# Placing two x tiles' transposes around one slot's second products, and bounding VectorE's background ahead of transposes

## The chip, the core and the metric

The kernel runs on one core of one Trainium2 chip. The time is the device time of one launch in microseconds (us), the median of several runs. TensorE multiplies matrices into PSUM, VectorE and ScalarE compute element by element and empty PSUM, GpSimd does small side work, and SyncE issues transfers. Each engine works through its own queue in order and waits on semaphores for the others.

## The reference

`x` is 2048 x 576 in float32. One normalised copy of it feeds an attention with a dilated window and a dense layer with ReLU, and both results are added to `x`.

```python
xn = layernorm(x)                                  # 2048 x 576
q, k, v = split(xn @ wqkv)                         # 32 heads of 18
# a position s sees s, s-2, ..., s-14 (8 keys); positions before 0 are masked
attn = softmax(q . k[s - 2*w] * 18 ** -0.5)
A = (attn . v[s - 2*w]) @ wo                       # 576 x 576
B = relu(xn @ w1) @ w2                             # 576 x 4608, 4608 x 576
out = x + A + B
```

## The kernel before

Each float32 operand of a matmul is split into a high and a low part, and a product takes three terms (high by high, high by low, low by high). `two` (L158, L160, L162) does so for weights: ScalarE copies the high part, VectorE (or, for a few, GpSimd) subtracts it from the source.

The positions are worked in two phases (`ph`) of eight tiles of 128 rows. A phase has 144 slots: 12 chunks of 384 columns of `w1`, and in each chunk 4 pairs of x tiles (`tb`) by 3 blocks of 128 columns (`f`). Slot `n` emits, for all engines, in this order:

- `run_splits`: weights that are due are split.
- `h_two`: TensorE's first products, `x` by `w1`, for the pair of slots two ahead. In an even slot this is the first half (28 matmuls), in an odd one the second (26), and then `h_out` brings the two results out of PSUM: ScalarE writes `hhi` (L559), VectorE writes `hlo` (L562). The results lie in two tiles called `ph` or two called `pm`.
- the work in `todo`, put there by `at`: first products of the attention (`qkv_tile`), loads, statistics, norms, transposes.
- `o_two`: TensorE's second products, `h` by `w2` (24 matmuls, more where `wo` is multiplied in), into four tiles `po`. Every third slot `o_out` adds them to `x` on VectorE (L674).
- the work in `todo_late`, put there by `late`.
- `run_bg`: VectorE's background, which is the attention's element-wise work (`attention` puts it in the queue `bg`: L439 and L442 for the logits, L471 for the products with `v`, L478 for their sums). An operation is taken as long as a running estimate of VectorE's time does not pass TensorE's by more than `margin(n)`.

All matmuls (L125) run as pairs, one on each half of TensorE's rows. PSUM has two tiles `pm`. They serve the pairs of first products, the attention's first products, and all transposes by `turn_rows` (L354), of which one call takes both tiles: 10 small matmuls.

Transposes come from two places. `make_xt_rows` turns a normalised tile of the next phase's `x`; ScalarE (L340, L341) and VectorE (L342, L343) then empty the two tiles `pm` into `xT`, one half each. `wo_parts` turns a finished tile of the attention's result; ScalarE (L520) and VectorE (L521, L522) empty it into a tile `k` and a tile `xn`, and slots 266, 269, 272 and 275 multiply them by `wo`.

The steps of the next phase's tiles stand in `XT_STEPS`, one row for each tile: the slots of its load, its statistics (`stats`), its norm (`norm`, three ScalarE instructions, L283, L284, L289) and its transposes, counted from slot 132. So tile 0 is transposed in slot 135, tiles 1 and 2 both in slot 136, tile 3 in slot 142, tiles 4 and 5 in slots 144 and 145, tiles 6 and 7 in 147 and 148. `wo_parts` of the second phase stand in slots 264, 265, 267, 268, 270, 271, 273 and 274.

`busy_m` is the set of all slots that use `pm` for transposes or for the attention's first products. `margin` reads it, and so does `h_two`, which then doesn't take `pm`. In each phase the attention's last unit leaves its background to the slots just before and among the `wo_parts`.

Of the kernel before, what the change touches and what calls it, by code (L numbers as in the profile page):

```python
# [33 lines left out]

XT_STEPS = (
    (-6, 0, 1, 3), (-5, 0, 2, 4), (-3, 1, 3, 4), (4, 6, 7, 10),
    (4, 6, 8, 12), (7, 9, 10, 13), (8, 12, 13, 15), (10, 13, 14, 16),
)
WO_STEPS = (-2, -1)
HEADW = (-9, -8, -7, -6, -5, -4)  # L40
# [16 lines left out]
def tile_body(ctx: ExitStack, tc: tile.TileContext, x, wqkv, wo, w1, w2, out):  # L57
# [440 lines left out]
    def run_bg(margin):  # L498

        ran = False  # L500
        while bg and t["dve"] + bg[0][0] / 960.0 <= t["pe"] + margin and not (ran and bg[0][0] == 0):
            n, f, a = bg.popleft()
            f(*a)
            if n:
                ran = True
                dve(n)
# [179 lines left out]
    def at(n, f, *a):  # L686
        todo.setdefault(n, []).append((f, a))
# [3 lines left out]
    def late(n, f, *a):  # L691
        todo_late.setdefault(n, []).append((f, a))

    plan = []
    busy_m = set()
    for ph in range(NPH):
        b = ph * SPP
        for c in range(NCH):
            for f in range(C):
                s = b + c * SPC + f  # L700
                first = ph == c == 0
                plan.append((HEADW[f] if first else s + (-5, -5, -4)[f], w1_task, ((ph, c, f), c * C + f)))
                plan.append((HEADW[3 + f] if first else s + (-3, -2, -2)[f], w2_task, ((ph, c, f), c * C + f)))
        for u in range(NU):
            s = b + UNIT0[ph] + u * UNIT_STEP
            plan.append((s - 5, wq_tasks, ((ph, u), u)))
            for i in range(NI):
                at(s + i, qkv_tile, ph, u, i)
                busy_m.add(s + i)
            at(s + NI, halos, ph, u)  # L710
            late(s + NI + 1, attention, ph, u)
        plan.append((b + WO_CHUNK * SPC - 6, wo_tasks, (ph,)))
        for i in range(NI):
            z = b + WO_CHUNK * SPC + C * (i // 2) + C - 1
            at(z + WO_STEPS[i % 2], wo_parts, ph, i)
            busy_m.add(z + WO_STEPS[i % 2])
        if ph + 1 < NPH:
            e = b + SPP - SPC
            for i in range(NI):
                load, sums, normed, parts = (e + k for k in XT_STEPS[i])  # L720
                at(load, load_x, ph + 1, i)
                at(sums, stats, ph + 1, i, False, True)
                at(normed, norm, ph + 1, i, True)
                at(parts, make_xt_rows, ph + 1, i)
                busy_m.add(e + XT_STEPS[i][-1])
    for step, f, a in sorted(plan, key=lambda z: z[0]):
        if f in (wq_tasks, wo_tasks):
# [85 lines left out]
        late((4, 4, 6, 7)[tb], twin, tb)  # L813
    def margin(n):

        odd, qkv = n % 2 == 0, n + 1 in busy_m
        due = sum(z[0] <= n + 1 for z in (*staged, *tasks))
        if slots[n][3] == 1:
            return (1.8 if odd else 2.7 + 2.4 * qkv) - 0.8 * due + 1.6 * (odd and qkv)
        return (2.5 if odd else 3.5 + 2.4 * qkv) - 0.8 * due + 1.6 * (odd and qkv)  # L820

    for n in range(FIRST, len(slots)):
        if n == ROW0:
            AHEAD["n"] = 4
        run_splits(n)
        g = n - n % 2 + LAG
        if n < ROW0:
            h_mm(n + LAG)
        elif g < len(slots):
            h_two(g, n % 2 == 1)  # L830
        for f, a in todo.pop(n, []):
            f(*a)
        if ROW0 - 1 <= n < len(slots) - C:
            o_two(n)
        else:
            o_mm(n, n != HALVED)
        if n == HALVED:
            o_out(n, (0,))
        for f, a in todo_late.pop(n, []):
            f(*a)  # L840
        if n == HALVED:
            o_out(n, (1,))
        run_bg(margin(n))
# [27 lines left out]
```

## Time and profile before

| what | value |
|---|---|
| median of 3 runs | 1162.11 us (1159.17 to 1163.46) |
| the profiled execution | 1162.3 us, span 1160.5 us |
| TensorE busy | 1150.2 us, 99% of the span |
| VectorE busy | 795.4 us, 69% |
| ScalarE busy | 295.4 us, 25% |
| granted TensorE clock, mean | 0.997 of full speed |

The profile comes from one execution. PE is TensorE, PEld its loading of weights, DVE is VectorE, ACT is ScalarE, POOL is GpSimd, SP is SyncE. "L354" is line 354 of the kernel. The ends of matmuls are modelled, so short waits between them can hide in what counts as busy, and the time from one start to another is the better measure. The granted clock is the share of full speed that the hardware gave TensorE.

### The profile page before, as it was taken

Reading aid. Unit: us, or ns where it says so; the run is one execution under the profiler, and the core shown is the slowest. Engines: PE = TensorE matmul, PEld = TensorE weight load, DVE = VectorE, ACT = ScalarE, POOL = GpSimd, SP = SyncE. Lnnn points to the kernel's source line nnn. Section 1 sums busy time; section 2 is a strip of 40 time slices with the busy share of each in tenths; the row PEclk is TensorE's granted clock in tenths of the full one; section 3 lists DMA queues with packets and bytes.
Section 4 is the critical chain, followed back from the end, with each engine's and each line's share of the span. In section 5 each row is a group of like instructions: output and inputs, shape, how many; then the busy total and the mean of one; then the engine's idle time right before and its main releaser. Section 6 shows DMA issues by size and latency. Waiting matters only on the chain.

```text
span 1160.5 us, 38715 instructions
## 1 busy us (share of the span) xinstructions
PE 1150.2 (99%) x17334; PEld 1143.6 (99%) x17334; DVE 795.4 (69%) x1465; ACT 295.4 (25%) x796; POOL 55.7 (5%) x80
## 2 busy tenths in 40 slices
PE   9999999999999999999999999999999999999998
PEld 8999999999999999999999999999999999999998
DVE  7427787877787789534564178868868877896333
ACT  5322222221222222222552122222222222231110
POOL 3200000000000000000010000000000000011000
PEclk9999999999999999999999999999999999999999
DMA  6302312221221212301333033032121303221002
GB/s 185 99 21 80 85 35 66 77 66 47 72 68 52 77 39 59 116 25 44 113 96 97 2 100 93 16 92 70 47 65 48 96 14 100 56 80 51 12 2 84
DMA packets 85238, 76.75 MB, mean 66 GB/s; under 512 B 6624, under 2 KB 68832, under 8 KB 85072
## 3 DMA queue, kind: packets, MB, share of 16 engines
q1 hardware_dynamic: 84640, 73.82, 22.3%
q8 instruction: 136, 2.23, 0.8%
q10 hardware_dynamic: 432, 0.46, 0.1%
q14 instruction: 30, 0.25, 0.1%
HBM read 61.34 MB, written 4.72 MB: 57 GB/s over the span
## 4 chain that ended last, share of the span: by engine, by line
PE 97%; DVE 1%; ACT 1%; issue 0%; DMA 0%; POOL 0%; DVEq 0%; ACTq 0%
PE po L125 43%; PE pm L125 26%; PE ph L125 25%; PE ph L115 1%; PE po L115 1%; PE pm L354 1%; DVE x L674 0%; PE pm L302 0%; DMA x<-in_x 0%; PE pm L115 0%; ACT xn L283 0%; DVE bst L263 0%; DVE pr L471 0%; DVE hlo L562 0%; ACT xT L307 0%
## 5 line engine op out<-in xcount | busy, mean ns | idle before, releaser
L125 PE MATMUL po<-w2t,hhi 64*128 64x256 f32 (+1 forms) x4448 | 449.4, 293 | 0.0
L125 PEld LDWEIGHTS po<-w2t,hhi 64*128 64x128 f32 x4448 | 359.0, 185 | 0.6
L125 PE MATMUL po<-w2t,hlo 64*128 64x256 f32 (+1 forms) x2224 | 334.8, 291 | 0.0
L125 PE MATMUL ph<-xT,w1t 64*128 64x256 f32 x5076 | 324.8, 275 | 0.0
L125 PEld LDWEIGHTS ph<-xT,w1t 64*128 64x128 f32 x5076 | 313.5, 185 | 0.7 <-DVE hlo L562 0.2
L674 DVE TENSOR_TENSOR x<-po,x 128x320 f32<-128x320 f32 (+1 forms) x384 | 149.7, 449 | 174.3 <-PE po L125 171.6
L125 PEld LDWEIGHTS po<-w2t,hlo 64*128 64x128 f32 x2224 | 217.7, 186 | 0.0
L125 PE MATMUL pm<-wq,xT 64*128 64x432 f32 x1728 | 179.3, 354 | 0.0
L559 ACT ACTIVATE hhi<-ph 128x256 fp32r<-128x256 f32 x197 | 65.4, 381 | 421.4 <-PE ph L125 409.2
L125 PEld LDWEIGHTS pm<-wq,xT 64*128 64x128 f32 x1728 | 159.9, 184 | 3.3
L125 PE MATMUL pm<-xT,w1t 64*128 64x256 f32 x2430 | 153.4, 273 | 0.0
L125 PEld LDWEIGHTS pm<-xT,w1t 64*128 64x128 f32 x2430 | 148.3, 184 | 0.0
L562 DVE SCALAR_TENSOR_TENSOR hlo<-ph,hhi 128x256 fp32r<-128x256 f32 x197 | 74.5, 417 | 105.7 <-ACT hhi L559 105.6
L439 DVE TENSOR_TENSOR pr<-qo,k 128x1152 f32<-128x1152 f32 x64 | 85.6, 1349 | 4.1 <-DMA k<-k 4.1
L559 ACT ACTIVATE hhi<-pm 128x256 fp32r<-128x256 f32 x91 | 30.0, 382 | 222.1 <-PE pm L125 222.1
L471 DVE TENSOR_TENSOR pr<-lg,v 128x1152 f32<-128x1152 f32 x64 | 84.7, 1349 | 0.2
L442 DVE TENSOR_REDUCE lg<-pr 128x64 f32<-128x1152 f32 x64 | 84.8, 1342 | 0.0
L478 DVE TENSOR_TENSOR pr<-pr 128x288 f32<-128x288 f32 (+1 forms) x128 | 69.9, 597 | 0.0
L162 DVE TENSOR_TENSOR w2t<-st,w2t 128x576 fp32r<-128x576 f32 x72 | 53.8, 747 | 9.8 <-ACT w2t L158 9.6
L562 DVE SCALAR_TENSOR_TENSOR hlo<-pm,hhi 128x256 fp32r<-128x256 f32 x91 | 34.3, 418 | 37.2 <-ACT hhi L559 36.2
L162 DVE TENSOR_TENSOR w1t<-st,w1t 128x640 fp32r<-128x640 f32 x70 | 57.2, 817 | 3.5 <-ACT w1t L158 3.1
L406 ACT ACTIVATE k<-pm 128x144 f32<-128x144 f32 x64 | 19.3, 302 | 146.8 <-PE pm L125 119.5
(86 smaller groups left out, 716.1 us busy)
## 6 DMA issues: line engine op xcount, KB each, us to landing
st<-in_w SPq DMA_DIRECT2D x72, 288.0 KB, 3.0
st<-in_w SPq DMA_DIRECT2D x72, 256.0 KB, 3.0
st<-in_wqkv SPq DMA_DIRECT2D x32, 216.0 KB, 3.0
st<-in_w SPq DMA_DIRECT2D x144, 32.0 KB, 2.7
out<-x SPq DMA_DIRECT2D x15, 288.0 KB, 2.4
x<-in_x SPq DMA_DIRECT2D x14, 288.0 KB, 4.2
k<-k SPq DMA_DIRECT2D x8, 441.0 KB, 3.9
v<-v SPq DMA_DIRECT2D x8, 441.0 KB, 4.5
```

The source lines that it names most:

```text
L115: nc.tensor.matmul(o, l, r, start=start, stop=stop)
L125: ins = nc.tensor.matmul(o, l[z], r[z], start=start, stop=stop)
L162: nc.vector.tensor_tensor(lo, src, f32(hi), op=ALU.subtract)
L354: nc.tensor.transpose(pt[:, k], src[rows, k * P : (k + 1) * P], ident[rows, rows])
L406: nc.scalar.activation(k[:, W - 1 + j, :], pq[:, 1, :], AF.Copy)
L439: nc.vector.tensor_tensor(pr[i], q, window(k, i), op=ALU.mult)
L442: nc.vector.tensor_reduce(lg[:, i], pr.pop(i).rearrange(heads, d=Dh), axis=AX.X, op=ALU.add)
L471: nc.vector.tensor_tensor(pr[i].rearrange(heads, d=Dh), e, window(v, i).rearrange(heads, d=Dh), op=ALU.mult)
L478: nc.vector.tensor_tensor(o, z[:, 0:n], z[:, n : 2 * n], op=ALU.add)
L559: nc.scalar.activation(hi, pt, AF.Relu)
L562: nc.vector.scalar_tensor_tensor(lo, pt, 0.0, f32(hi), op0=ALU.max, op1=ALU.subtract)
L674: nc.vector.tensor_tensor(acc[:, cols], PO[k, h], acc[:, cols], op=ALU.add)
```

## The change

Three edits, each a line or two.

- Where two tiles have their transposes in the same slot, the second one's go to `todo_late`, behind that slot's second products. This holds for tile 2 in slot 136 alone.
- The norm of tile 5 moves from slot 142 to slot 143.
- `margin(n)` treats only slots with the attention's first products as before. Ahead of any other slot in `busy_m` (those with transposes) it is 1.4.

```diff
-    (4, 6, 8, 12), (7, 9, 10, 13), (8, 12, 13, 15), (10, 13, 14, 16),
+    (4, 6, 8, 12), (7, 9, 11, 13), (8, 12, 13, 15), (10, 13, 14, 16),
 ...
+    qkv_slots = set()
 ...
                 at(s + i, qkv_tile, ph, u, i)
                 busy_m.add(s + i)
+                qkv_slots.add(s + i)
 ...
                 at(normed, norm, ph + 1, i, True)
-                at(parts, make_xt_rows, ph + 1, i)
+                (late if i and XT_STEPS[i - 1][-1] == XT_STEPS[i][-1] else at)(parts, make_xt_rows, ph + 1, i)
                 busy_m.add(e + XT_STEPS[i][-1])
 ...
     def margin(n):
-        odd, qkv = n % 2 == 0, n + 1 in busy_m
+        odd, qkv = n % 2 == 0, n + 1 in qkv_slots
+        if n + 1 in busy_m and not qkv:
+            return 1.4
         due = sum(z[0] <= n + 1 for z in (*staged, *tasks))
         if slots[n][3] == 1:
             return (1.8 if odd else 2.7 + 2.4 * qkv) - 0.8 * due + 1.6 * (odd and qkv)
         return (2.5 if odd else 3.5 + 2.4 * qkv) - 0.8 * due + 1.6 * (odd and qkv)
```

In the order in which the engines' queues are then written, no instruction is added or removed. TensorE's differs in slot 136 alone. ScalarE's differs by the one norm. VectorE's differs in slots 264 to 268 alone (elsewhere no background is left where the new `margin` holds, or none comes out otherwise):

```
before                                     after
L478 x2, L478 x2 (sums of tiles 4, 5)      w2t split
L471 x2 (products of tiles 6, 7)           tile 0 of wo_parts: L521, L522 x2
w2t split                                  L478 x2, L478 x2 (sums of tiles 4, 5)
tile 0 of wo_parts: L521, L522 x2          hlo x2
L478 (sum)                                 tile 1 of wo_parts
hlo x2                                     L471 (product of tile 6)
tile 1 of wo_parts                         L674 x4
L674 x4                                    hlo x2
L478 x5 (sums of tiles 6, 7)               tile 2, tile 3 of wo_parts
hlo x2                                     L471 (product of tile 7)
tile 2, tile 3 of wo_parts                 L478 x6 (sums of tiles 6, 7)
```

## The prediction

> **What bounds the kernel now.** I read the page's shares first, then the chain of waits that ended last, then TensorE's own waits, and then the order of time around those waits on four engines.
>
> ```profile
> PE 1150.2 (99%) x17334; PEld 1143.6 (99%) x17334; DVE 795.4 (69%) x1465; ACT 295.4 (25%) x796; POOL 55.7 (5%) x80
> PE 97%; DVE 1%; ACT 1%; issue 0%; DMA 0%; POOL 0%; DVEq 0%; ACTq 0%
> PE pm L354 <- DVE xT L343: 1.9, 2, 1.4
> PE pm L354 <- DVE xn L522: 1.7, 2, 1.3
> ```
>
> TensorE is busy for 1150.2 of 1160.5 us, and the chain is 97% TensorE. The change adds and removes no matmul, so only the time in which TensorE stands, or runs slowly, can come back. The last two rows (total us, times, longest us) say where it stands in mid-kernel: twice ahead of transposes at L354, each time because VectorE has not yet emptied the PSUM tile `pm` that the transposes write. That is 3.6 us, and by itself only 0.3%. The order of time shows more. Columns are start, duration, engine, line, tiles, count; a duration includes a modelled tail, so I measure from start to start.
>
> ```profile
> 556.24 0.48 PE L125 MATMUL po<-w2t,hhi 64*128 64x256 f32 x4
> ...
> 557.91 1.76 PE L125 MATMUL ph<-xT,w1t 64*128 64x256 f32 x28
> 559.50 0.47 PE L354 MATMUL pm<-ident,xn 64*128 64x64 f32 x10
> 561.39 0.24 PE L354 MATMUL pm<-ident,xn 64*128 64x64 f32 x1 [1.42 <-DVE xT L343]
> 562.08 0.74 PE L354 MATMUL pm<-ident,xn 64*128 64x64 f32 x9 [0.45 <-DVE xT L343]
> 562.53 0.82 PE L125 MATMUL po<-w2t,hhi 64*128 64x256 f32 x4
> ...
> 565.55 1.68 PE L125 MATMUL ph<-xT,w1t 64*128 64x256 f32 x26
> ```
>
> This is slot 136. Its first products of `h` (28 matmuls) take 559.50 - 557.91 = 1.59 us, then both x tiles 1 and 2 are transposed back to back, then come its second products (24 matmuls on `po`). In the slot before, those 24 took 557.91 - 556.24 = 1.67 us; behind the wait they take 565.55 - 562.53 = 3.02. The other wait looks alike, at slot 265 (transposes of attention tile 1):
>
> ```profile
> 1052.34 1.67 PE L125 MATMUL ph<-xT,w1t 64*128 64x256 f32 x26
> 1055.30 0.24 PE L354 MATMUL pm<-ident,qo 64*128 64x64 f32 x1 [1.29 <-DVE xn L522]
> 1055.99 0.50 PE L354 MATMUL pm<-ident,qo 64*128 64x64 f32 x9 [0.45 <-DVE xn L522]
> 1056.27 0.51 PE L125 MATMUL po<-w2t,hhi 64*128 64x256 f32 x4
> ...
> 1058.65 2.67 PE L125 MATMUL ph<-xT,w1t 64*128 64x256 f32 x28
> 1061.11 0.44 PE L125 MATMUL po<-w2t,hhi 64*128 64x256 f32 x4
> ```
>
> Behind it, second products take 2.38 us and the next first products 2.46 instead of 1.59. The windows view gives the reason. The last three columns are granted clock, DMA share, GB/s:
>
> ```profile
> 562.10:562.20 0.10, 0.10 (x3) 0.10 (x5) 0.00 (x0) 0.00 (x0) 0.00 (x0) 0.65 0.70 276
> 565.50:565.60 0.10, 0.10 (x5) 0.10 (x4) 0.00 (x0) 0.00 (x0) 0.00 (x0) 0.79 0.00 0
> 1057.00:1057.10 0.10, 0.10 (x6) 0.10 (x4) 0.10 (x2) 0.10 (x1) 0.00 (x0) 0.80 0.00 0
> 1060.40:1060.50 0.10, 0.10 (x5) 0.10 (x4) 0.00 (x0) 0.00 (x0) 0.00 (x0) 0.63 0.00 0
> 5.00:10.00 5.00, 3.86 (x26) 3.05 (x25) 3.49 (x10) 4.32 (x8) 3.34 (x5) 1.00 0.86 244
> ```
>
> The clock falls at about 562.1 and returns at about 565.5; it falls at 1057.1 and returns at 1060.4: 3.4 us both times, and 495 us apart, 145 times 3.41. So it looks as if the clock is decided on a fixed grid of 3.41 us by what TensorE did in one such window, and costs half the window when it falls. Each gap thus costs twice: the standing, then the slow matmuls. The last row is for later: 1.14 us idle in 5 us at the kernel's head, clock 1.00.
>
> **Slot 136: the transposes of tile 2 move behind the second products.** In the changed order TensorE goes on at 559.50 + 0.28 (ten transposes, from 1055.99 to 1056.27) = 559.78 with the 24 second products, until 561.45. What then lets the transposes of tile 2 start is VectorE's emptying of tile 1, two halves:
>
> ```profile
> 561.01 0.23 DVE L343 TENSOR_TENSOR xT<-pm,xT 64x64 fp32r<-64x64 f32 x1
> ...
> 561.71 0.23 DVE L343 TENSOR_TENSOR xT<-pm,xT 64x64 fp32r<-64x64 f32 x1
> ```
>
> The halves end at 561.24 and 561.94, and TensorE went on 0.15 us behind each (561.39, 562.08). The change does not speed these up: they hang on ScalarE's copies of tile 1, which keep their place. So the first transpose goes at 561.45 at once and the second still waits until 562.08. A rest of 562.08 - 561.45 = 0.63 us stays. The standing falls from 562.08 - 559.78 = 2.30 to 0.63: **1.67 us back**. The next products of `h` then start at 562.08 + 0.28 = 562.36 if the clock holds, against 565.55, so together 3.19 come back and **the clock's part is 1.52**. Cover: tile 2's own copies now end later relative to TensorE. Tile 1's ended 561.94 - 559.78 = 2.2 us behind its transposes; so counted, tile 2's end at 562.36 + 2.2 = 564.5, and their `pm` is next written by slot 138's first products, at 562.36 + 1.49 + 1.67 = 565.5 (1.49 for 26 matmuls, of the 1.59 for 28). That leaves 1.0 us; if it were gone, `pm` would be waited for there. VectorE and ScalarE keep their queue order here, and no DMA moves.
>
> **Slot 265: VectorE's background.** What VectorE did while TensorE waited:
>
> ```profile
> 1051.21 2.66 DVE L471 TENSOR_TENSOR pr<-lg,v 128x1152 f32<-128x1152 f32 x2
> ...
> 1055.62 0.23 DVE L522 TENSOR_TENSOR xn<-pm,k 64x64 fp32r<-64x64 f32 x1
> ```
>
> Two background products of 1.33 us stood ahead of the emptying (L521, L522) of attention tile 0, with a weight split between. `margin` gave 5.9 and 4.1 at the ends of slots 263 and 264, less 0.8 for each weight due; it is now 1.4, and the planned order puts that tile's four instructions straight behind the weight split, ahead of all of this background. The emptying ended at 1055.85; without the 2.66 us alone it ends by 1053.2. TensorE is ready for the transposes at 1052.34 + 1.49 = 1053.83, so it waits for nothing. Standing removed: 1055.99 - 1053.83 = **2.16 us**. Slow matmuls: (2.38 - 1.67) + (2.46 - 1.59) = **1.58 us**. The background does not vanish: one L471 now runs in slot 265, another with six sums (L478) behind the emptying of tile 3 in slot 268. What is late next there is the pair `hlo` behind that block:
>
> ```profile
> L471 DVE TENSOR_TENSOR pr<-lg,v 128x1152 f32<-128x1152 f32 x64 | 84.7, 1349 | 0.2
> L478 DVE TENSOR_TENSOR pr<-pr 128x288 f32<-128x288 f32 (+1 forms) x128 | 69.9, 597 | 0.0
> 1077.34 0.23 DVE L522 TENSOR_TENSOR xn<-pm,k 64x64 fp32r<-64x64 f32 x1
> 1085.18 0.76 DVE L674 TENSOR_TENSOR x<-po,x 128x256 f32<-128x256 f32 x2 [5.17 <-PE po L125]
> ```
>
> The block is at most 1.35 + 6 x 0.60 = 4.9 us. From 1077.57 to VectorE's next bound work at 1085.18 are 7.6 us, so it fits with 2.7 to spare, and `hlo` (0.76) too. Cost nothing; without that cover, up to 4.9.
>
> **Norm of tile 5 one slot later.** ScalarE's three instructions of this norm move from ahead of slot 143's `hhi` to behind it.
>
> ```profile
> 586.26 0.42 PE L125 MATMUL po<-w2t,hhi 64*128 64x256 f32 x4
> 588.01 2.20 PE L125 MATMUL ph<-xT,w1t 64*128 64x256 f32 x28
> 589.96 0.46 PE L354 MATMUL pm<-ident,xn 64*128 64x64 f32 x8
> 586.04 0.67 ACT L158 ACTIVATE w2t<-st 128x576 fp32r<-128x576 f32 x1
> 587.53 0.76 DVE L562 SCALAR_TENSOR_TENSOR hlo<-ph,hhi 128x256 fp32r<-128x256 f32 x2
> ```
>
> Second and first products took 589.96 - 586.26 = 3.70, against 1.67 + 1.59 = 3.26: a hidden loss of 0.44 us, as `ph` was freed by `hlo` only at 588.29. `hlo` was late because ScalarE's norm delayed the weight split (586.04), and VectorE's half of that split stood ahead of `hlo`. With the norm away the split is done early and `hlo` ends about 0.6 earlier. **I take 0.4 back**, bounds 0 and 0.44. The norm's transposes stand two slots on, some 6.5 us by these rows, and nothing else reads it: it would have to end later than that to be felt.
>
> **Sum.** 3.19 + 3.74 + 0.4 = 7.3 us. Against the profiled execution's 1162.3 (span 1160.5 and 1.8 around it) that gives **1155.0**. The median of the runs shown, 1162.11, is 0.2 below that execution, so I keep 1155.0. The lowest run, 1159.17, is 3.1 below the profiled one, which is just the clock's part (1.52 + 1.58): it may be an execution in which the grid cut both gaps and the clock held. There only 4.2 come back, which again ends at 1155.0. This supports the forecast, but is an inference.
>
> **The rivals.** (a) The 0.63 us left in slot 136 still lowers the clock. Against it: the 1.14 us idle at the head left it at 1.00; for it: nobody has shown the limit between 1.14 and the 2.16 that did lower it. Price 1.5: 1156.5. (b) The slow spells are not caused by these gaps and come anyway: then only 1.67 + 2.16 + 0.4 = 4.2 come back, 1158.1. The Trainium skill speaks for it: "TensorE: Matmul & The Clock Gate", section "What's actually happening", has the half clock come after at least one idle window of about 3.4 us, and by that rule gaps of some 2.2 us would not lower it. The trace agrees with the page's half rate and with its free-running window of 3413 ns, but here the clock fell right behind the only two gaps of this kind, which speaks against the rule's limit. (c) The change does not reach the waits: a transposed tile still meets a VectorE that is late, and everything stays: 1162. Against it stands the planned order, which moves exactly the named instructions. (d) Slower: the background, held back in slots 263 to 267, is paid out ahead of later evictions, and transposes of slots 270 to 274 wait in its place. It decides once the block exceeds the 7.6 us found above; each such wait costs what slot 265's did, 3.74, and four of them give 1155.0 + 15.0 = 1170.0. At 4.9 us the block is far from it.
>
> **How the numbers follow.** A measurement of this kernel tells about 0.5% (5.8 us) from no change, so "faster" means below 1156.3. Forecast 0.74, its own range 1153.0 to 1157.0 (the runs shown spread by 4.3, half of it either side); (a) 0.10; (b) 0.08; (c) 0.04; (d) 0.04. The range from 1153.0 to 1158.3 takes in the forecast, (a) and (b) and leaves out about 0.15. Faster: four fifths of the forecast and half of (a), 0.65; slower 0.03, the rest 0.32.
>
> **What would show it.** Right: no TensorE wait at L354 for L522, one of about 0.45 us for L343; granted clock 1.00 from 40 us on; the 24 second products behind slot 265's transposes at 1.67 us; slot 143's `hlo` ahead of TensorE. Wrong: a spell of clock 0.50 behind slot 136, a wait of TensorE for `hlo` or `xT` in slots 137 to 139 or 268 to 271, or a time above 1158.3.

## The result and the profile after

The changed kernel takes **1157.73 us** (median of 6, 1154.82 to 1158.04) against 1162.11 for the kernel before (median of 6 as well, 1159.17 to 1163.46): ratio 0.9962, 95% interval 0.9947 to 0.9978. It is faster by 0.4%, and less than the 0.5% set as the bound for "faster". The forecast was 1155.0 with a range of 1153.0 to 1158.3.

The profiled execution took 1154.82 us (span 1153.0), 7.5 less than the profiled one before, where the sum had said 7.3. The median fell by 4.4 only. Executions of both kernels fall into two groups some 3 us apart, and the two medians are not made up of the same ones: of the changed kernel the profiled execution is in the lower group and the five others, at 1157.54 to 1158.04, are in the upper one.

The page's first lines, and TensorE's waits (engine, line, waited for: us in total, times, longest us):

```profile
span 1153.0 us, 38714 instructions
PE 1145.1 (99%) x17334; PEld 1139.6 (99%) x17334; DVE 795.9 (69%) x1465; ACT 295.6 (26%) x796; POOL 53.4 (5%) x80
...
PE pm L354 <- DVE xT L343: 0.4, 1, 0.4
```

The two waits of 1.9 and 1.7 us have become one of 0.4. No wait for L522 is left. TensorE's order of time at slot 136 (start, duration, engine, line, tiles, count):

```profile
557.82 1.76 PE L125 MATMUL ph<-xT,w1t 64*128 64x256 f32 x28
559.41 0.47 PE L354 MATMUL pm<-ident,xn 64*128 64x64 f32 x10
559.69 0.47 PE L125 MATMUL po<-w2t,hhi 64*128 64x256 f32 x4
...
561.33 0.22 PE L354 MATMUL pm<-ident,xn 64*128 64x64 f32 x1
561.99 0.49 PE L354 MATMUL pm<-ident,xn 64*128 64x64 f32 x9 [0.44 <-DVE xT L343]
562.27 1.81 PE L125 MATMUL ph<-xT,w1t 64*128 64x256 f32 x26
```

Tile 1's transposes are followed at once by the second products. Tile 2's first transpose goes at 561.33 and the second waits until 561.99. The next products start at 562.27; this execution was 0.09 us ahead of the other already, so the forecast of 562.36 is met exactly. Slot 265 and slots 143 and 144:

```profile
1048.65 1.68 PE L125 MATMUL ph<-xT,w1t 64*128 64x256 f32 x26
1050.14 0.50 PE L354 MATMUL pm<-ident,qo 64*128 64x64 f32 x10
1050.42 0.51 PE L125 MATMUL po<-w2t,hhi 64*128 64x256 f32 x4
...
1052.10 1.79 PE L125 MATMUL ph<-xT,w1t 64*128 64x256 f32 x28
```

```profile
583.05 0.41 PE L125 MATMUL po<-w2t,hhi 64*128 64x256 f32 x4
...
584.63 1.81 PE L125 MATMUL ph<-xT,w1t 64*128 64x256 f32 x28
586.25 0.49 PE L354 MATMUL pm<-ident,xn 64*128 64x64 f32 x10
```

The transposes of slot 265 wait for nothing, and the second products behind them take 1052.10 - 1050.42 = 1.68 us, where they took 2.38. Slot 143's second and slot 144's first products take 586.25 - 583.05 = 3.20 us, where they took 3.70. The windows view around both old gaps shows the clock (third column from the right) at 1.00:

```profile
558.00:564.00 6.00, 5.56 (x100) 5.41 (x100) 2.73 (x9) 3.22 (x11) 0.00 (x0) 1.00 0.38 101
1046.00:1052.00 6.00, 6.00 (x110) 6.00 (x108) 4.86 (x15) 2.08 (x6) 0.45 (x2) 1.00 0.27 79
```

### The profile page after: what moved, and what is told of

Same layout as the page of the kernel before. It is cut to its first block, busy times and chain, and to the rows that moved or that the text cites. A ratio compares the mean times of both kernels' runs of the same rounds, so it can differ in the third digit from the quotient of the medians.

```text
span 1153.0 us, 38714 instructions
## 1 busy us (share of the span) xinstructions
PE 1145.1 (99%) x17334; PEld 1139.6 (99%) x17334; DVE 795.9 (69%) x1465; ACT 295.6 (26%) x796; POOL 53.4 (5%) x80
## 4 chain that ended last, share of the span: by engine, by line
PE 97%; DVE 1%; issue 1%; DMA 1%; ACT 1%; POOL 0%; DVEq 0%; POOLq 0%; ACTq 0%
PE po L125 43%; PE pm L125 27%; PE ph L125 25%; PE pm L354 1%; PE po L115 0%; PE ph L115 0%; DMA x<-in_x 0%; DMA st<-in_w 0%; DMA st<-in_wqkv 0%; DVE bst L263 0%; POOL rstd L270 0%; DVE x L674 0%; ACT xn L283 0%; DVE w2t L162 0%; PE pm L302 0%
## 5 line engine op out<-in xcount | busy, mean ns | idle before, releaser
L674 DVE TENSOR_TENSOR x<-po,x 128x320 f32<-128x320 f32 (+1 forms) x384 | 149.7, 449 | 169.1 <-PE po L125 166.4
```

Source lines behind the costliest of these rows:

```text
L674: nc.vector.tensor_tensor(acc[:, cols], PO[k, h], acc[:, cols], op=ALU.add)
```

## The experiments

Two things had to be settled: whether each part of the sum belongs to its edit, and where the other 3 us of the median come from. "The lower group" and "the upper group" are the two groups of times. Each run gives the mean granted clock of each execution; one half-clock spell of 3.41 us in mid-kernel brings it to 0.998, sometimes 0.999, two to 0.997 or 0.996; the group and the spells together give the time.

### The changed kernel again

No edit.

> The changed kernel itself, unchanged, to see where its executions differ: its profiled execution took 1154.82 us, its other five 1157.5 to 1158.0. My theory: the 3 us lie in the kernel's head (the first 45 us), where the clock starts at half rate and turns full at some point of a fixed grid; from 45 us on every execution runs alike. Then the times again fall into 1154 to 1158, and a profiled execution above 1156 shows its extra time ahead of 45 us and a granted clock of 1.00 from there to the last matmul. Rival: a half-clock spell behind the 0.63 us that is left in slot 136 comes in most executions; then a profiled execution above 1156 shows a clock of 0.50 near 562 us.

Median 1157.93 us against 1163.62 of the kernel before (23 executions on the same chip), ratio 0.9949 (0.9937 to 0.9962). The profiled execution took 1155.21, the four others 1157.80 to 1158.14, all with clock 1.000: the rival of a spell behind slot 136 falls. But the profiled execution was again of the lower group, so it did not show where the 3 us lie; the theory that they lie in the kernel's head is tested by a trace of the upper group further down.

The kernel before shows the same groups, and the clock sorts its executions. On this chip and the next: at 1.000, about 1159.2 or 1162.2; at 0.998, about 1160.8 or 1163.9; at 0.997, about 1162.3 or 1165.3. So a spell costs 1.6 to 1.7 us, and both groups exist without the change. The profiled execution of before, with its two spells, is of the lower group (1159.2 and two spells of 1.6): 1162.3 there and a median of 1162.11 agree by accident.

### The late transposes alone

```diff
-                at(parts, make_xt_rows, ph + 1, i)
+                (late if i and XT_STEPS[i - 1][-1] == XT_STEPS[i][-1] else at)(parts, make_xt_rows, ph + 1, i)
```

> The kernel before with one edit of the change: tile 2's transposes behind slot 136's second products. My theory: TensorE's time up to slot 138 is 1.67 us shorter where the clock did not fall there before, 3.2 us where it did; slot 265 keeps its wait of 1.7 us and, in an execution whose grid does not cut that gap, its half-clock spell of 3.4 us. Profiled execution 1159.1 against 1162.3, or 1157.5 if the clock holds at slot 265 too. Rival (the half-clock spells come whatever TensorE waits for): a spell of 0.50 still stands near 562 us and only 1.7 us come back.

Median 1158.11 us, ratio 0.9956 (0.9945 to 0.9968); profiled 1157.82, near the 1157.5 expected where the clock holds at both places. TensorE reaches slot 138 3.1 us earlier than in the profiled execution of before, whose clock had fallen there. Slot 265 keeps its wait, and the clock holds there. The windows are those of the clock's grid; the first number behind the length is TensorE's busy time:

```profile
1052.30 0.24 PE L354 MATMUL pm<-ident,qo 64*128 64x64 f32 x1 [1.32 <-DVE xn L522]
1053.00 0.49 PE L354 MATMUL pm<-ident,qo 64*128 64x64 f32 x9 [0.46 <-DVE xn L522]
...
1048.44:1051.85 3.41, 2.54 (x42) 2.34 (x39) 3.41 (x4) 0.89 (x3) 2.52 (x2) 1.00 0.01 1
1051.85:1055.26 3.41, 2.50 (x40) 2.43 (x42) 3.24 (x10) 0.77 (x2) 0.00 (x0) 1.00 0.32 87
```

The grid cut this gap into two halves, and neither window lost enough. All five executions but one (1159.34, clock 0.998) are within 0.3 us; had one of them been of the upper group, it would have stood near 1161.

### The bound on the background alone

```diff
+        if n + 1 in busy_m and not qkv:
+            return 1.4
```

(with `qkv` read from the attention's slots, as in the change)

> The kernel before with one edit of the change: the bound of 1.4 on VectorE's background. My theory: slot 265's wait goes (2.16 us) and with it any half-clock spell there (1.6 us); slot 136 keeps its waits of 1.4 and 0.45 us. Profiled execution 1158.6, with a spell of 0.50 near 562 us if the grid does not cut that gap. Rival (spells come anyhow): a spell of 0.50 stands near 1054 us without a wait ahead of it.

Median 1159.76 us, ratio 0.9970 (0.9960 to 0.9981); 12 executions spread over four places: three at 1156.9 to 1157.2, two near 1158.5, three near 1159.9, four near 1161.6, as two groups with and without one spell must. The profiled one took 1157.17, not the 1158.6 expected with a spell near 562 us: no wait in slot 265, both waits in slot 136, and the clock held there because the grid cut that gap too:

```profile
558.29:561.70 3.41, 1.99 (x39) 1.88 (x36) 1.38 (x5) 2.25 (x7) 0.00 (x0) 1.00 0.34 92
561.70:565.11 3.41, 2.96 (x50) 2.85 (x52) 1.76 (x6) 0.97 (x4) 0.00 (x0) 1.00 0.31 87
```

So the standing time comes back where its edit is, each time, and the clock's part only where the clock had fallen. In neither trace is there a spell where the gap is gone, so the rivals of both runs fall.

### The later norm alone

```diff
-    (4, 6, 8, 12), (7, 9, 10, 13), (8, 12, 13, 15), (10, 13, 14, 16),
+    (4, 6, 8, 12), (7, 9, 11, 13), (8, 12, 13, 15), (10, 13, 14, 16),
```

> The kernel before with one edit of the change: the norm of tile 5 one slot later. My theory: the first products of slot 144 start 0.4 us earlier relative to slot 142, nothing else moves, and the time does not tell it from the kernel before (ratio 0.998 to 1.002). Rival: the norm's delay costs its transposes in slot 145 a wait, and the slot is no earlier.

Median 1161.52 us, ratio 0.9982 (0.9974 to 0.9991). Slot 143's second and slot 144's first products:

```profile
584.81 0.41 PE L125 MATMUL po<-w2t,hhi 64*128 64x256 f32 x4
...
586.39 1.77 PE L125 MATMUL ph<-xT,w1t 64*128 64x256 f32 x28
587.98 0.48 PE L354 MATMUL pm<-ident,xn 64*128 64x64 f32 x10
```

587.98 - 584.81 = 3.17 us instead of 3.70: the norm's edit brings 0.5, and no wait shows at slot 145's transposes. The medians differ by more (2.1 us), but they mix groups and spells. This trace is also the only one of an execution that its time puts into the upper group (1161.52). Its clock is 1.00 up to 1158 us and it has no wait that the others lack. It loses 2.9 us between 608 and 1043 us, spread over that whole time, so not in the kernel's head as I had supposed. The windows view, this kernel first, then the kernel before:

```profile
700.00:800.00 100.00, 100.00 (x1500) 100.00 (x1498) 79.18 (x132) 24.58 (x71) 2.75 (x3) 1.00 0.22 62
800.00:900.00 100.00, 100.00 (x1502) 100.00 (x1500) 80.07 (x134) 23.73 (x68) 2.74 (x3) 1.00 0.23 63
```

```profile
700.00:800.00 100.00, 100.00 (x1511) 99.84 (x1510) 79.89 (x131) 23.54 (x68) 2.75 (x3) 1.00 0.22 61
800.00:900.00 100.00, 100.00 (x1510) 99.84 (x1508) 80.67 (x135) 24.70 (x70) 2.74 (x3) 1.00 0.23 64
```

1500 matmuls in 100 us instead of 1511: some 0.7% less. Read start by start, the two matmuls of a pair (one on each row half) start mostly 5 to 50 ns apart there, and the distance changes from pair to pair; the other traces so far keep a steady 3 or 10 ns. The next theory takes it for a larger distance that lasts.

### A fresh start of both row halves

```diff
+    def drain():
+        tc.add_manual_dep(nc.tensor.nop().ins, LAST[0].ins.name, SYNC, reason="both row halves start anew")
...
+    for n in (150, 152):
+        at(n, drain)
```

(`LAST[0]` is the last matmul issued)

> The changed kernel, with a wait in slots 150 and 152: TensorE's second products there start only when its first products are done, so both row halves start anew. Theory S (skew): most executions of the changed kernel take 3 us more than its profiled one because TensorE's two row halves run the second phase 13 to 49 ns apart instead of 3 to 9, as the norm-only kernel's trace shows (it loses 2.9 us between 608 and 1043 us, evenly, at full clock), and a fresh start near 620 us puts them right: every execution at 1155.0 to 1156.0 (two waits cost 0.2 to 0.5 us). Rival D: the 3 us come from something that the start of both halves does not touch (transfers, the taking of the profile): executions stay at 1157.5 to 1158.5. Rival R: the skew is drawn anew at each start: executions fall into both groups.

Median 1156.35 us of 9, ratio 0.9957 (0.9941 to 0.9973): five at 1155.5 to 1156.4, four at 1158.4 to 1158.8. That is as rival R has it. Five of nine in the lower group, against two of seven in the next run on the same chip, which has no such wait, is too few to say that the wait helps. The two waits themselves cost 0.8 us by this trace (more than the 0.2 to 0.5 expected): from slot 146 to slot 160 it takes 61.36 us, and the changed kernel's second trace 60.60.

### Tile 2's transposes one slot later still

```diff
-    (-6, 0, 1, 3), (-5, 0, 2, 4), (-3, 1, 3, 4), (4, 6, 7, 10),
+    (-6, 0, 1, 3), (-5, 0, 2, 4), (-3, 1, 3, 5), (4, 6, 7, 10),
```

> The changed kernel with tile 2's transposes one slot later still, in slot 137 behind its first products. My theory of the 0.63 us that is left in slot 136: tile 1's copies end 2.2 us behind its transposes, and first products (1.49 us) more lie between now, so no wait is left at L343 and TensorE is 0.6 us earlier at slot 138. Rival: tile 2's copies now stand ahead of the sums of slot 137 on VectorE, and the second products of slot 138 wait for these: the 0.6 us are lost again. Either way the time stays within 0.1% of the changed kernel.

Median 1157.55 us, ratio 0.9956 (0.9939 to 0.9973); lower group 1154.5, upper 1157.5 to 1157.8. The wait for L343 is gone, and the rival came with it. TensorE and VectorE in slot 138:

```profile
566.55 0.45 PE L125 MATMUL po<-w2t,hhi 64*128 64x256 f32 x4
566.78 0.33 PE L125 MATMUL po<-w2t,hlo 64*128 64x256 f32 x2
566.90 0.96 PE L125 MATMUL po<-w2t,hhi 64*128 64x320 f32 x4
...
568.61 1.67 PE L125 MATMUL ph<-xT,w1t 64*128 64x256 f32 x26
565.69 1.55 DVE L674 TENSOR_TENSOR x<-po,x 128x256 f32<-128x256 f32 x4
```

Second products of 568.61 - 566.55 = 2.06 us instead of 1.6: VectorE's copies of tile 2 now stand ahead of its sums (L674, ending at 567.2), and TensorE's matmuls on the two `po` that are summed last (the `64x320` rows) wait for these, hidden in a duration of 0.96 instead of 0.47. Of the 0.63 us, 0.2 are still there at slot 140.

### Pauses of known length

The pauses stand in 19 slots; each adds GpSimd instructions that TensorE waits for, so the time as such says nothing.

```diff
+    def pause(k):
+        for j in range(k):
+            z = nc.gpsimd.memset(pause_tile, 0.0)
+            if j == 0:
+                tc.add_manual_dep(z.ins, LAST[0].ins.name, SYNC, reason="pause starts behind the matmuls")
+        tc.add_manual_dep(nc.tensor.nop().ins, z.ins.name, SYNC, reason="pause ends")
...
+        at(n, pause, 3 + j)
```

> The changed kernel with 19 pauses of TensorE in the first phase, in every fourth slot outside the attention's first products, each as long as a chain of 3 to 21 small GpSimd instructions (about 0.7 to 3.5 us). It measures the clock by itself. My theory: the clock is decided on a fixed grid of 3.41 us, and falls to half for one window where a window had more idle time than some limit between 1.1 and 1.7 us; so pauses under 1.1 us never lower it, long ones do for 3.41 us, and between 1.2 and 2.2 us it hangs on how the grid cuts the pause. Rival (a rule of one whole idle window): only pauses of 3.4 us and more lower it.

The pauses came out at 1.0 to 4.6 us, measured from the last start ahead of a pause to the first behind it. Each window is one of the clock's grid, and the row behind it, where there is one, the next:

```profile
192.06:195.47 3.41, 2.10 (x32) 2.13 (x34) 1.26 (x1) 0.00 (x0) 0.86 (x7) 1.00 0.25 76
205.71:209.12 3.41, 1.67 (x28) 1.49 (x26) 0.52 (x1) 0.00 (x0) 1.10 (x8) 1.00 0.24 65
209.12:212.53 3.41, 3.41 (x59) 3.41 (x58) 2.93 (x8) 1.14 (x3) 0.00 (x0) 1.00 0.02 5
...
219.37:222.78 3.41, 1.47 (x28) 1.30 (x24) 3.41 (x6) 0.00 (x0) 1.24 (x9) 1.00 0.02 6
222.78:226.19 3.41, 3.41 (x29) 3.41 (x31) 0.76 (x1) 0.00 (x0) 0.00 (x0) 0.50 0.30 65
...
297.87:301.28 3.41, 2.28 (x38) 2.07 (x35) 1.61 (x3) 0.00 (x0) 0.71 (x6) 1.00 0.85 241
301.28:304.69 3.41, 2.21 (x34) 2.24 (x36) 1.29 (x2) 0.00 (x0) 0.81 (x6) 1.00 0.02 7
304.69:308.10 3.41, 3.41 (x60) 3.41 (x59) 1.80 (x5) 1.29 (x3) 0.00 (x0) 1.00 0.03 7
```

In this trace a window with 1.47 us busy lowers the clock for the whole next one, and a window with 1.67 does not. A pause of 2.2 us that lies in one window (219.37) costs a spell, one of 2.6 us that is cut in two (297.87, 301.28) costs none. All ten pauses from 2.8 us on lowered it; each left a window with at most 1.18 us busy. The limit that I expected, 1.1 to 1.7 us idle, was somewhat low; the rule of a whole idle window falls.

The two gaps of the kernel before bound the limit from the other side. Each of their windows is followed by the half-clock one:

```profile
558.72:562.13 3.41, 1.54 (x31) 1.32 (x28) 1.30 (x4) 1.72 (x6) 0.00 (x0) 1.00 0.42 100
562.13:565.54 3.41, 3.41 (x33) 3.41 (x35) 1.30 (x4) 0.97 (x4) 0.00 (x0) 0.50 0.16 64
1053.65:1057.06 3.41, 1.67 (x30) 1.39 (x28) 3.29 (x9) 1.22 (x4) 0.32 (x1) 1.00 0.31 87
1057.06:1060.47 3.41, 3.41 (x34) 3.41 (x33) 1.57 (x6) 0.21 (x1) 0.00 (x0) 0.50 0.02 5
```

Here a window with 1.67 us lowered the clock; in the pauses' trace one with the same 1.67 did not. As the ends of matmuls are modelled, the busy time of a window is not good to the last digit; the traces place the limit near 1.67 us of work and no closer.

### One more small matmul on one row half

```diff
+            if g == 154:
+                o, l, r, start, stop, n = runs[0][0]
+                nc.tensor.matmul(o[:, 0:64], l[0:64], r[0:64, 0:64], start=True, stop=True)
```

> The changed kernel with one more small matmul (64 columns, about 27 ns, its result written over by the next) on the first row half alone, ahead of slot 152's first products. Theory S (TensorE's two row halves keep the distance at which they last were set, and 13 to 49 ns cost about 3 us over the second phase): the trace shows another distance than 3 or 9 ns from about 625 us on, and its phase runs slower by up to 3 us, without a wait and at full clock; the shares of the two groups of times (about 1155 and 1158) change. Rival D (the 3 us have nothing to do with the distance): distance changed, second phase as long as before; two groups as in the changed kernel.

The same on the second half (`runs[1][0]`, rows 64 to 127):

> The same with the small matmul on the second row half. Theory S: the distance changes the other way, so that one of the two kernels has more slow executions than the changed kernel and the other fewer, or both more; a profiled execution near 1158 shows a distance over 13 ns through the second phase, one near 1155 a distance of 3 or 9. Rival D: no such link between distance and time in these traces.

And the changed kernel beside them:

> The changed kernel once more as the control for the two. Either theory: times in two groups near 1155 and 1158, three quarters of them in the upper; half of the lower group's distance to the kernel before (4.2 us, group by group) from the waits that went, none from the clock in executions of either that held it.

Medians 1154.97, 1154.91 and 1154.94 us against 1160.71, ratios 0.9952, 0.9951 and 0.9951 (0.9938 to 0.9963 for the control). On this chip no execution of any kernel is of the upper group, which no expectation had foreseen: all 15 of these three lie within 1154.7 and 1155.2, so the shares of the groups could not be compared. In the first trace the pairs start 3 ns apart, a distance that other runs have too. In the second trace the pairs start 23 ns apart through the whole second phase, and it runs as fast as ever, 1510 matmuls in 100 us:

```profile
800.00:900.00 100.00, 100.00 (x1510) 100.00 (x1509) 79.73 (x132) 24.77 (x70) 2.74 (x3) 1.00 0.24 66
```

So a distance that stays the same does not cost the 3 us, and theory S falls as I had put it.

The pauses' trace shows more, in its second phase, long behind the last pause and at clock 1.00. From the first products of slot 161 to those of slot 256 it takes 364.54 us, just what the later norm's trace takes there, and in both the distance changes from pair to pair. The twelve other traces keep one distance through almost all of this stretch (3, 10 or 23 ns) and take 361.95 to 362.08 us. So the slow rate goes along with a changing distance; which of the two brings the other, no run shows.

### The later transposes and the changed kernel side by side

> The kernel with tile 2's transposes in slot 137 again, beside the changed kernel on one chip. Expected from its first trace: 0.16 us less on TensorE in all (0.63 us of wait gone, most of it given back by slot 139), so 0.1 to 0.4 us less in time, group by group; if the control is as fast, the wait left in slot 136 is worth nothing.

> The changed kernel as the control. Where executions of it take about 1158 on this chip, executions of the kernel before should stand in groups 3 us apart too (1159.2 and 1162.1 at a clock of 1.000, 1.6 more for each half-clock spell); where none does, none of the kernel before's should: the 3 us then belong to the chip or the execution and not to the change.

1157.49 us (1154.71 and 1157.42 to 1157.60) and 1157.79 (1154.90 and 1157.64 to 1158.01), against 1163.50 (1159.46 to 1164.23); ratios 0.9957 (0.9941 to 0.9973) and 0.9955 (0.9940 to 0.9971). Group by group the later transposes are 0.2 to 0.3 us faster; no more than that is left in slot 136. Both kernels, changed and before, show the two groups on this chip: the 3 us belong to the chip or the execution, and not to the change.

## Why the prediction was right, and where it was not

**Slot 136.** Right to 0.1 us: 3.19 worked out; less the 0.09 us of lead, 3.19 measured at the next first products and 3.11 by slot 140, with the remaining wait at the foretold place and of the foretold 0.45 us (0.44).

**Slot 265.** Right: 3.74 worked out, 3.69 measured at the start of slot 267, by when both slow pieces of before are past. The emptying of attention tile 0 ended ahead of the transposes as forecast.

**The norm.** 0.4 worked out, 0.5 measured, alone and in the change, and by the foretold way. This is slot 143's `hlo` after:

```profile
583.69 0.76 DVE L562 SCALAR_TENSOR_TENSOR hlo<-ph,hhi 128x256 fp32r<-128x256 f32 x2 [0.91 <-ACT hhi L559]
```

It starts 583.69 - 583.05 = 0.64 us behind the first of the slot's second products, where it started 587.53 - 586.26 = 1.27 behind. My bound of 0.44 was a little low because I took 1.67 us for second products that take 1.58 where no transposes stand ahead of them.

**The block in slot 268.** VectorE's order of time after:

```profile
1069.94 1.36 DVE L471 TENSOR_TENSOR pr<-lg,v 128x1152 f32<-128x1152 f32 x1
1071.21 2.16 DVE L478 TENSOR_TENSOR pr<-pr 128x576 f32<-128x576 f32 x4
1073.29 0.52 DVE L478 TENSOR_TENSOR qo<-pr 128x144 f32<-128x144 f32 x2
1073.84 0.76 DVE L562 SCALAR_TENSOR_TENSOR hlo<-ph,hhi 128x256 fp32r<-128x256 f32 x2
1077.51 0.75 DVE L674 TENSOR_TENSOR x<-po,x 128x256 f32<-128x256 f32 x2 [2.92 <-PE po L125]
```

3.9 us instead of at most 4.9, and VectorE still waits 2.92 us for TensorE behind it: the cover held, and rival (d) stayed far off.

**What the sum left out.** Another 0.3 us came back by slot 269: the background no longer stands ahead of `hlo` in slot 267. In the profile of before, slot 268's first products take 1075.08 - 1073.30 = 1.78 us and not 1.59, behind a `hlo` that stood behind five sums. I had passed this over as small.

**The clock.** The reading of two gaps that cost twice was right, and so was the grid. Rival (a) did not come: the window that holds the 0.63 us (560.57 to 563.98) had 2.97 us busy. Rival (b) was wrong as a mechanism: the pauses lower the clock by themselves. The Trainium skill's "TensorE: Matmul & The Clock Gate", section "What's actually happening", agrees with the traces on the half rate (0.50), on the window of 3413 ns (each fall here lasts 3.41 us or twice that) and on its running free (the grid cut slot 265's gap in one trace and not in another). It differs on what lowers the clock: it asks for an idle window, and here a window with 1.47 us of work, of 3.41, was enough.

**The step that failed** is the one from the profiled execution to the median: "The median of the runs shown, 1162.11, is 0.2 below that execution, so I keep 1155.0." The equality was an accident. The profiled execution had two spells (3.1 us) and was of the lower group; most others had one spell or none, and many were of the upper group, 3 us longer. Of the 7.5 us only 4.3 are there in every execution (1159.2 to 1154.9 at clock 1.000, lower group; 1162.2 to 1157.9, upper group), and 1.6 more for each spell that the kernel before suffers. I had written down this alternative for the lowest run and drew the right conclusion for the lower group (1154.67 to 1155.21 is what these executions take), but not that the kernel as a whole has another one. That 1157.73 still lies within 1153.0 to 1158.3 is luck: the forecast's own range ended at 1157.0, and the wider one was there for rivals (a) and (b), of which neither came. That (b)'s 1158.1 is so near has one plain reason: where the clock had held before, only the 4.2 us of standing come back, as (b) had counted, and the median of before is about what an execution of the upper group takes without a spell. So the time missed by 2.7 us, and the chance of 0.65 for "faster" looks too high: the ratios of the changed kernel's four measurements are 0.9962, 0.9949, 0.9951 and 0.9955, on both sides of the bound of 0.995.

**What stays open** is the cause of the upper group. Shown are: it is at full clock; it appears with and without the change; on one of four chips it never came in 24 executions; in the one trace of it, the loss of 2.9 us is spread over the second phase, with no wait. The same slow rate stands in the pauses' trace, and in both traces the distance between the row halves changes all the time. A steady 23 ns costs nothing; whether a changing distance causes the loss, or only comes with it, was not tried.

## What to carry to other kernels

Where TensorE is busy for 99%, look for its few gaps of over a microsecond and at the clock behind them: here a gap of 2.2 us cost its length, and some 1.6 us more if it left one window of the clock more than half idle. A wait for an engine's queue is ended by taking away what stands ahead of the awaited instruction or by putting other work of the waiting engine between, and both can be read from start times to 0.1 us. But a forecast made against one profiled execution needs that execution's own place in the spread first: list what in it is particular (its spells, its group) and take it out of both sides before the difference is put against the median.

## What the hardware showed that I had not expected

- The clock's window has a limit near half: at full clock, windows with 1.47, 1.54 and 1.67 us busy of 3.41 lowered it, another one with 1.67 did not, and 1.99 and more never did. The fall lasts exactly one window, 3.41 us, behind most pauses up to 4.56 us. Only those of 3.97 and 4.36 us cost two: they reached into the half-clock window and left it 2.33 and 2.14 us busy, where 3.06 let the clock return.
- The same queue of matmuls at full clock, without waits, took 0.7% longer over 435 us in one execution than in the others, and at the same rate in part of another; in both, the distance in time between the two row halves kept changing. The whole kernel has two groups of times 3 us apart on three of four chips.
